# A low-rank decode-attention kernel: longer rows per load, a two-chunk ring, tapered last loads and an early softmax phase

## The chip, the cores and the metric

The kernel runs on one core of a Trainium2 chip. The metric is device time in microseconds (us). The kernel before takes 337.39 us (median of 6 runs, 337.14 to 338.04). A profile covers the span from the first to the last instruction, which is some 1.8 us shorter than the measured time. Engine names in the profile: PE is TensorE (matmuls), PEld its weight loads, DVE is VectorE, ACT is ScalarE, POOL is GpSimd, SP is SyncE; a "q" after a name is that engine's sequencer, for example while it issues a DMA. The granted PE clock is the share of TensorE's full clock that the profile records as granted.

## The reference, cut to what matters

```
B, H, Sq, Skv, Dh, R = 1, 16, 1, 8192, 256, 16          # everything in bf16
kp = einsum("rn,bhnd->bhrd", e_proj, k)                  # [16 heads, 16, 256]
vp = einsum("rn,bhnd->bhrd", f_proj, v)
scores = einsum("bhqd,bhrd->bhqr", q, kp) * (Dh ** -0.5)
p = softmax(scores, axis=-1)                             # over 16 values
o = einsum("bhqr,bhrd->bhqd", p, vp)
```

K and V are 67.1 MB each, and every byte is used once. Everything else is small: after the two projections only 16 x 256 numbers are left per head.

## The kernel before

Partition p holds positions n = 64 p to 64 p + 63 of a head, so a head of K is a tile of 128 partitions by 64 "columns" of 256 numbers, and one partition's 64 columns are 32 KB in one piece of memory. A chunk is some of these columns. Each column is one matmul (128 x 16 weights from e_proj, 128 x 256 of K).

```
CC_MAIN = 16        # columns per chunk: a 1 MB load with 8 KB per partition
CC_LAST = 8         # last head: 512 KB, 4 KB per partition
NB = 10             # ten K buffers and ten V buffers
...
# SP issues K (ACT issues V in the same way)
for i, (h, c0, c1) in enumerate(chunks):
    b = i % NB
    if i >= NB:
        sp.wait_ge(sem_kd, i - NB + 1)          # TensorE is done with this buffer
    sp.dma_start(kbuf[b][:, 0:(c1 - c0) * D], kv_src(kt, h, c0, c1)).then_inc(semK[b], 16)
...
# TensorE: K chunk, V chunk, K chunk, ...; after the last of them
pe.wait_ge(sem_dve, 7)                          # the softmax of all 16 heads is there
pe.wait_ge(sem_dvv, H)
for h in range(H):                              # 16 output matmuls
    mm = pe.matmul(ps_o[0:H, :], ptm[0:R, h * H:(h + 1) * H], vp_bf[0:R, h * D:(h + 1) * D],
                   start=(h == 0), stop=(h == H - 1))
...
# VectorE: one multiply-and-reduce with q per head, then once for all heads: transpose, max,
# scale, (exp on ScalarE), reciprocal, multiply, transpose, product with a block mask
```

## Time and profile before

| | before |
|---|---|
| measured median | 337.39 us |
| span of the profile | 335.6 us |
| PE busy | 241.1 us (72%) |
| bytes read | 134.87 MB, 421 GB/s from 20 to 240 us |
| mean granted PE clock | 0.987 |

From the page of the kernel before: the span, and three lines of the strip of 40 equal slices (busy tenths of PE, granted PE clock in tenths, GB/s that the DMA engines moved).

```profile
span 335.6 us, 4413 instructions
PE   0767867767767767866866787766866866867875
PEclk9998999999999999999999899999999999999999
GB/s 220 422 422 419 422 419 422 422 419 422 419 422 421 420 422 419 422 419 423 422 421 421 418 423 419 422 419 422 422 419 423 419 422 424 418 420 408 411 338 7
```

PE is never full and its clock is almost always granted. The load rate is flat at 418 to 424 GB/s from the second slice to the 36th, then 408 to 411 in the last head, whose rows are 4 KB long instead of 8 KB. That is the picture of a kernel bound by its load stream.

The end of the chain that ended last, in order of time (start us, us, what):

```profile
297.12 29.81 DMA vbuf<-in_v_dram
326.94 0.04 issue
326.98 1.04 PE vp_ps L206 x8
328.02 0.87 PE kp_ps L194 x8
328.89 0.89 PE vp_ps L206 x8
...
329.80 0.37 ACT vp_bf L157
330.18 0.30 ACT e L176 x2
...
331.51 1.92 PE ps_o L217 x16
333.43 0.02 issue
333.45 0.37 ACT o_sb L182
```

The chain leaves the DMA at 326.94 us. Then come three groups of eight matmuls, the softmax, 16 output matmuls, a copy, and the store to 335.6.

### The profile page before, as it was taken

To read this page: it belongs to the slowest core of one execution; us is meant where nothing else is said; L and a number is where in the kernel's file an instruction comes from. 1 tells how busy PE (TensorE), PEld (TensorE's weight loads), DVE (VectorE), ACT (ScalarE), POOL (GpSimd) and SP (SyncE) were. 2 spreads that over 40 slices of the span, in tenths; PEclk is the share of its full clock that TensorE was granted. 3 is DMA by queue.
4 is the path that set the end of the run, shared out by engine and by line. 5 is a ranking of instruction groups with operands and counts; after the bars stand their busy time and mean duration, and the time that the engine had idled before them with its cause. 6 is when DMAs were issued, how large, how long until landed. Compare 5 with 4: busy or idle time off the path is not lost.

```text
span 335.6 us, 4413 instructions
## 1 busy us (share of the span) xinstructions
PE 241.1 (72%) x2064; PEld 182.5 (54%) x2064; DVE 10.2 (3%) x45; ACT 8.1 (2%) x21; POOL 1.6 (0%) x6
## 2 busy tenths in 40 slices
PE   0767867767767767866866787766866866867875
PEld 0554655555655655655655565655655645656653
DVE  2000000000000000000000000000000000000002
ACT  0100000000000000000000000000000000000001
POOL 1000000000000000000000000000000000000000
PEclk9998999999999999999999899999999999999999
DMA  8999999999999999999999999999999999999980
GB/s 220 422 422 419 422 419 422 422 419 422 419 422 421 420 422 419 422 419 423 422 421 421 418 423 419 422 419 422 422 419 423 419 422 424 418 420 408 411 338 7
DMA packets 23793, 135.16 MB, mean 403 GB/s; under 512 B 6336, under 2 KB 6352, under 8 KB 8400
## 3 DMA queue, kind: packets, MB, share of 16 engines
q1 hardware_dynamic: 11920, 67.51, 49.0%
q10 hardware_dynamic: 11856, 67.38, 48.8%
q8 instruction: 16, 0.26, 0.3%
q14 instruction: 1, 0.01, 0.0%
HBM read 134.87 MB, written 0.01 MB: 402 GB/s over the span
## 4 chain that ended last, share of the span: by engine, by line
DMA 91%; PE 6%; ACTq 1%; ACT 0%; issue 0%; DVE 0%
DMA vbuf<-in_v_dram 91%; PE vp_ps L206 5%; ACTq L168 1%; PE kp_ps L194 1%; PE ps_o L217 1%; ACTq L149 0%; ACT vp_bf L157 0%; ACT o_sb L182 0%; ACT e L176 0%; DVE ptm L262 0%; DVE p L257 0%; DVE pt L259 0%; DVE stats L255 0%; ACTq L156 0%
## 5 line engine op out<-in xcount | busy, mean ns | idle before, releaser
L206 PE MATMUL vp_ps<-vbuf,f_sb 128*16 128x256 bf16 x1024 | 125.5, 276 | 80.6 <-DMA vbuf<-in_v_dram 80.6
L206 PEld LDWEIGHTS vp_ps<-vbuf,f_sb 128*16 128x16 bf16 x1024 | 87.9, 90 | 117.2 <-DMA vbuf<-in_v_dram 78.3
L194 PE MATMUL kp_ps<-kbuf,e_sb 128*16 128x256 bf16 x1024 | 125.4, 276 | 10.0 <-DMA kbuf<-in_k_dram 10.0
L194 PEld LDWEIGHTS kp_ps<-kbuf,e_sb 128*16 128x16 bf16 x1024 | 93.3, 91 | 31.0 <-issue 9.9
L238 DVE CUSTOM_DVE_ANT_0 junk<-kp_ps,q_bc 16x256 f32<-16x256 f32 x16 | 6.6, 412 | 314.4 <-PE kp_ps L194 314.4
L157 ACT ACTIVATE vp_bf<-vp_ps 16x256 bf16<-16x256 f32 x16 | 6.0, 373 | 309.1 <-PE vp_ps L206 309.1
L217 PE MATMUL ps_o<-vp_bf,ptm 16*16 16x256 bf16 x16 | 1.9, 268 | 1.7 <-DVE ptm L262 1.7
L217 PEld LDWEIGHTS ps_o<-vp_bf,ptm 16*16 16x16 bf16 x16 | 1.3, 85 | 2.4 <-DVE ptm L262 2.0
L171 ACT ACT_TABLE_LOAD x1 | 1.3, 1283 | 13.6 <-issue 13.6
L232 DVE COPY e_sb<-e_raw 128x1024 bf16<-128x1024 bf16 x1 | 1.0, 1027 | 5.3 <-DMA f_raw<-in_f_proj_dram 5.3
L238 DVE DVE_READ_ACCUMULATOR2_ANT s<- 16x1 f32 x16 | 1.1, 71 | 0.0
L233 DVE COPY f_sb<-f_raw 128x1024 bf16<-128x1024 bf16 x1 | 1.0, 1023 | 0.0
L113 POOL MEMSET maskbd<- 32x1024 bf16 x1 | 0.9, 941 | 0.3 <-POOLq L281 0.3
L115 POOL TENSOR_SCALAR_AFFINE_SELECT maskbd<-maskbd 16x256 bf16<-16x256 bf16 x1 | 0.5, 496 | 0.2 <-POOL maskbd L113 0.2
L182 ACT ACTIVATE o_sb<-ps_o 16x256 bf16<-16x256 f32 x1 | 0.4, 373 | 3.0 <-PE ps_o L217 3.0
L176 ACT ACTIVATE e<-st,stats 16x16 f32<-16x16 f32 x1 | 0.3, 290 | 0.0
L262 DVE TENSOR_TENSOR ptm<-maskbd,pt 16x256 bf16<-16x256 bf16 x1 | 0.3, 278 | 0.0
L257 DVE TENSOR_SCALAR p<-e,stats 16x16 bf16<-16x16 f32 x1 | 0.2, 222 | 0.0
L171 ACT ACTIVATE warm<-warm 1x1 f32<-1x1 f32 x1 | 0.2, 202 | 0.0
L259 DVE STREAM_TRANSPOSE pt<-p 32x32 bf16<-32x32 bf16 x1 | 0.2, 200 | 0.0
L249 DVE STREAM_TRANSPOSE st<-s 32x32 f32<-32x32 f32 x1 | 0.2, 199 | 0.0
L176 ACT ACTIVATION_READ_ACCUMULATOR e<-st,stats 16x1 f32 x1 | 0.2, 185 | 0.0
(11 smaller groups left out, 1.1 us busy)
## 6 DMA issues: line engine op xcount, KB each, us to landing
vbuf<-in_v_dram ACTq DMA_DIRECT2D x60, 1024.0 KB, 48.0
kbuf<-in_k_dram SPq DMA_DIRECT2D x60, 1024.0 KB, 47.5
kbuf<-in_k_dram SPq DMA_DIRECT2D x8, 512.0 KB, 37.2
vbuf<-in_v_dram ACTq DMA_DIRECT2D x8, 512.0 KB, 36.0
e_raw<-in_e_proj_dram SPq DMA_DIRECT2D x1, 256.0 KB, 3.9
f_raw<-in_f_proj_dram ACTq DMA_DIRECT2D x1, 256.0 KB, 5.4
q_bc<-in_q_dram SPq DMA_DIRECT2D x1, 128.0 KB, 5.7
out_dram<-o_sb SPq DMA_DIRECT2D x1, 8.0 KB, 1.4
```

Source lines behind the costliest of these rows:

```text
L113: gp.memset(mask[:], 0.0).then_inc(sem_mask, 1)
L115: gp.affine_select(out=mask[0:R, 0:H * H], in_=mask[0:R, 0:H * H], pattern=[[1, H], [-1, H]], compare_op=ALU.not_equal, fill=1.0, base=0, ...
L157: act.activation(vp_bf[0:R, h * D:(h + 1) * D], vp_ps[h % 2][:, :], ACT.Copy,).then_inc(sem_dvv, 1)
L168: act.dma_start(vbuf[b][:, 0:(c1 - c0) * D], kv_src(vt, h, c0, c1)).then_inc(semV[b], 16)
L171: act.activation(warm[0:1, 1:2], warm[0:1, 0:1], ACT.Exp)
L176: act.activation(e32[0:H, 0:R], st32[0:H, 0:R], ACT.Exp, bias=stats[0:H, 1:2], scale=scale, accum_out=stats[0:H, 2:3],).then_inc(sem_exp, 1)
L194: mm = pe.matmul(kp_ps[hb][:, :], e_sb[:, c, :], kbuf[b][:, (c - c0) * D:(c - c0 + 1) * D], start=(c == 0), stop=(c == C - 1),)
L206: mm = pe.matmul(vp_ps[hb][:, :], f_sb[:, c, :], vbuf[b][:, (c - c0) * D:(c - c0 + 1) * D], start=(c == 0), stop=(c == C - 1),)
L217: mm = pe.matmul(ps_o[0:H, :], ptm[0:R, h * H:(h + 1) * H], vp_bf[0:R, h * D:(h + 1) * D], start=(h == 0), stop=(h == H - 1),)
L232: dve.tensor_copy(e_sb[:], e_raw[:].transpose([0, 2, 1]))
L233: dve.tensor_copy(f_sb[:], f_raw[:].transpose([0, 2, 1])).then_inc(sem_prep, 1)
L238: dve.tensor_tensor_reduce(out=junk[hb][:, :], in0=kp_ps[hb][:, :], in1=q_bc[:, h * D:(h + 1) * D], scale=1.0, scalar=0.0, op0=ALU.mult, o ...
```

## The change

Its intent has two parts. The stream: load whole heads (64 columns, 4 MB, 32 KB per partition) for heads 0 to 11, in a ring of 160 columns for K and another for V, where two 64-column chunks fit. The tail: taper the loads of the last four heads, down to four columns for the last V; run softmax and output for heads 0 to 14 while the last head still loads; and fold the scaling by 1/sum into the last copy.

The diff, cut to its core:

```diff
-CC_MAIN = 16
-CC_LAST = 8
-NB = 10
+CC_MAIN = 64
+K_TAIL = {12: [32, 32], 13: [32, 32], 14: [32, 16, 16], 15: [16, 16, 16, 16]}
+V_TAIL = {12: [32, 32], 13: [32, 32], 14: [32, 16, 16], 15: [16, 16, 8, 8, 8, 4, 4]}
+RING = 160
+NS = 10
+K_AT = {(15, 48): (15, 36)}      # TensorE takes K's last chunk before V's chunk at column 40
...
+    hbs = [H - 1, H] if H > 1 else [H]        # two phases: heads 0-14, then all 16
...
-        kbuf = [sb([P, CCMAX * D], bf16, f"kbuf{b}") for b in range(NB)]
+        kbuf = sb([P, RING * D], bf16, "kbuf")
...
-                    if i >= NB:
-                        sp.wait_ge(sem_kd, i - NB + 1)
-                    sp.dma_start(kbuf[b][:, 0:(c1 - c0) * D], kv_src(kt, h, c0, c1)).then_inc(semK[b], 16)
+                    if kneed[i]:                          # chunks that overlapped this place are consumed
+                        sp.wait_ge(sem_kd, kneed[i])
+                    sp.dma_start(kbuf[:, koff[i] * D:(koff[i] + c1 - c0) * D],
+                                 kv_src(kt, h, c0, c1)).then_inc(semK[i % NS], 16)
...
+                    # TensorE, after V's first chunk of head 15: the output matmuls of heads 0-14
+                    while state["phased"] < NPH - 1 and h >= hbs[state["phased"]] and c0 == 0:
+                        emit_final(state["phased"], last=False)
+                        state["phased"] += 1
...
-                act.activation(o_sb[0:H, :], ps_o[0:H, :], ACT.Copy).then_inc(sem_oc, 1)
+                act.activation(
+                    o_sb[0:H, :], ps_o[0:H, :], ACT.Copy, scale=stats[NPH - 1][0:H, 2:3],
+                ).then_inc(sem_oc, 1)
```

More of the change, by code (lines that the diff above doesn't have):

```diff
@@ L35, in bass_standalone__low_rank_proj_linformer__decode_kernel, with make, place @@
     scale = float(D) ** -0.5
-    chunks = []
-    for h in range(H):
-        cc = CC_LAST if h == H - 1 else CC_MAIN
-        cc = min(cc, C)
-        assert C % cc == 0
-        for c0 in range(0, C, cc):
-            chunks.append((h, c0, c0 + cc))
-    NCH = len(chunks)
-    CCMAX = max(c1 - c0 for (_, c0, c1) in chunks)
-    end_cnt = {}
-    for i, (h, c0, c1) in enumerate(chunks):
-        if c1 == C:
-            end_cnt[h] = i + 1
-    assert NB <= NCH
+    def make(tails):
+        out = []
+        for h in range(H):
+            c0 = 0
+            for cc in tails.get(h, [CC_MAIN] * (C // CC_MAIN)):
+                out.append((h, c0, c0 + cc))
+                c0 += cc
+            assert c0 == C
+        return out
+    def place(chunks):
+        offs, need, off = [], [], 0
+        for i, (h, c0, c1) in enumerate(chunks):
+            n = c1 - c0
+            if off + n > RING:
+                off = 0
+            dep = max([j + 1 for j in range(i)
+                       if offs[j] < off + n and off < offs[j] + chunks[j][2] - chunks[j][1]],
+                      default=0)
+            offs.append(off)
+            need.append(max(dep, i - NS + 1, need[-1] if need else 0))
+            off += n
+        return offs, need
+    kch, vch = make(K_TAIL), make(V_TAIL)
+    koff, kneed = place(kch)
+    voff, vneed = place(vch)
+    kend = {h: i + 1 for i, (h, c0, c1) in enumerate(kch) if c1 == C}
+    vend = {h: i + 1 for i, (h, c0, c1) in enumerate(vch) if c1 == C}
+    order = []
+    ki = vi = 0
+    while vi < len(vch):
+        if ki < len(kch) and K_AT.get(kch[ki][:2], kch[ki][:2]) <= vch[vi][:2]:
+            order.append(("k", ki))
+            ki += 1
+        else:
+            order.append(("v", vi))
+            vi += 1
+    hbs = [H - 1, H] if H > 1 else [H]
     qt, kt, vt, et, ft, ot = (q.tensor, k.tensor, v.tensor,
@@ L63, in sm @@
             return es.enter_context(nc.semaphore(name))
+        NPH = len(hbs)
         e_raw = sb([P, R, C], bf16, "e_raw")
@@ L72, in bass_standalone__low_rank_proj_linformer__decode_kernel @@
         s32 = sb([32, 32], f32, "s32")
-        st32 = sb([32, 32], f32, "st32")
-        e32 = sb([32, 32], f32, "e32")
-        p16 = sb([32, 32], bf16, "p16")
-        pt16 = sb([32, 32], bf16, "pt16")
-        mask = sb([32, 32 * 32], bf16, "maskbd")
-        ptm = sb([32, 32 * 32], bf16, "ptm")
-        stats = sb([32, 4], f32, "stats")
+        stx = [sb([32, 32], f32, f"st{p}") for p in range(NPH)]
+        ex = [sb([32, 32], f32, f"e{p}") for p in range(NPH)]
+        etx = [sb([32, 32], f32, f"et{p}") for p in range(NPH)]
+        ptm = [sb([32, H * H], bf16, f"ptm{p}") for p in range(NPH)]
+        mask = sb([32, H * H], bf16, "maskbd")
+        stats = [sb([32, 4], f32, f"stats{p}") for p in range(NPH)]
         warm = sb([32, 2], f32, "warm")
         o_sb = sb([32, D], bf16, "o_sb")
-        kbuf = [sb([P, CCMAX * D], bf16, f"kbuf{b}") for b in range(NB)]
-        vbuf = [sb([P, CCMAX * D], bf16, f"vbuf{b}") for b in range(NB)]
+        kbuf = sb([P, RING * D], bf16, "kbuf")
+        vbuf = sb([P, RING * D], bf16, "vbuf")
         kp_ps = [ps([R, D], f32, f"kp_ps{b}") for b in range(2)]
         vp_ps = [ps([R, D], f32, f"vp_ps{b}") for b in range(2)]
-        ps_o = ps([R if R >= H else H, D], f32, "ps_o")
+        ps_o = ps([32, D], f32, "ps_o")
         sem_ef = sm("sem_ef")
@@ L94, in bass_standalone__low_rank_proj_linformer__decode_kernel @@
         sem_dvv = sm("sem_dvv")
-        sem_dve = sm("sem_dve")
-        sem_exp = sm("sem_exp")
+        sem_dx = [sm(f"sem_d{p}") for p in range(NPH)]
+        sem_ex = [sm(f"sem_e{p}") for p in range(NPH)]
         sem_peo = sm("sem_peo")
@@ L99, in bass_standalone__low_rank_proj_linformer__decode_kernel @@
         sem_out = sm("sem_out")
-        semK = [sm(f"semK{b}") for b in range(NB)]
-        semV = [sm(f"semV{b}") for b in range(NB)]
+        semK = [sm(f"semK{b}") for b in range(NS)]
+        semV = [sm(f"semV{b}") for b in range(NS)]
         def kv_src(tensor, h, c0, c1):
@@ L134, in _ @@
                 ).then_inc(sem_q, 16)
-                for i, (h, c0, c1) in enumerate(chunks):
-                    b = i % NB
-                    if i >= NB:
-                        sp.wait_ge(sem_kd, i - NB + 1)
-                    sp.dma_start(kbuf[b][:, 0:(c1 - c0) * D], kv_src(kt, h, c0, c1)).then_inc(semK[b], 16)
+                for i, (h, c0, c1) in enumerate(kch):
+                    if kneed[i]:
+                        sp.wait_ge(sem_kd, kneed[i])
+                    sp.dma_start(kbuf[:, koff[i] * D:(koff[i] + c1 - c0) * D],
+                                 kv_src(kt, h, c0, c1)).then_inc(semK[i % NS], 16)
                 sp.wait_ge(sem_oc, 1)
@@ L152, in _ @@
                 ).then_inc(sem_ef, 16)
-                copied = 0
+                state = {"copied": 0, "phased": 0}
                 def emit_vp_copy(h):
-                    act.wait_ge(sem_vd, end_cnt[h])
+                    act.wait_ge(sem_vd, vend[h])
                     act.activation(
@@ L159, in emit_vp_copy @@
                     ).then_inc(sem_dvv, 1)
-                for i, (h, c0, c1) in enumerate(chunks):
-                    b = i % NB
-                    if i >= NB:
-                        act.wait_ge(sem_vd, i - NB + 1)
-                        while copied < H and end_cnt[copied] <= i - NB + 1:
-                            emit_vp_copy(copied)
-                            copied += 1
-                    act.dma_start(vbuf[b][:, 0:(c1 - c0) * D], kv_src(vt, h, c0, c1)).then_inc(semV[b], 16)
-                    if i == NB - 1:
-                        act.wait_ge(sem_prep, 1)
-                        act.activation(warm[0:1, 1:2], warm[0:1, 0:1], ACT.Exp)
@@ L172, in _, with emit_exp @@
-                while copied < H:
-                    emit_vp_copy(copied)
-                    copied += 1
-                act.wait_ge(sem_dve, 3)
-                act.activation(
-                    e32[0:H, 0:R], st32[0:H, 0:R], ACT.Exp,
-                    bias=stats[0:H, 1:2], scale=scale,
-                    accum_out=stats[0:H, 2:3],
-                ).then_inc(sem_exp, 1)
-                act.wait_ge(sem_peo, 1)
-                act.activation(o_sb[0:H, :], ps_o[0:H, :], ACT.Copy).then_inc(sem_oc, 1)
+                def emit_exp(pi):
+                    hb = hbs[pi]
+                    act.wait_ge(sem_dx[pi], 2)
+                    act.activation(
+                        ex[pi][0:hb, 0:R], stx[pi][0:hb, 0:R], ACT.Exp,
+                        bias=stats[pi][0:hb, 0:1], scale=1.0,
+                        accum_out=stats[pi][0:hb, 1:2],
+                    ).then_inc(sem_ex[pi], 1)
@@ new lines, in emit_ready_work @@
+                def emit_ready_work(cnt):
+                    while state["copied"] < H and vend[state["copied"]] <= cnt:
+                        emit_vp_copy(state["copied"])
+                        state["copied"] += 1
+                    while state["phased"] < NPH - 1 and state["copied"] >= hbs[state["phased"]]:
+                        emit_exp(state["phased"])
+                        state["phased"] += 1
+                warmed = False
+                for i, (h, c0, c1) in enumerate(vch):
+                    if vneed[i]:
+                        if not warmed:
+                            act.wait_ge(sem_prep, 1)
+                            act.activation(warm[0:1, 1:2], warm[0:1, 0:1], ACT.Exp)
+                            warmed = True
+                        act.wait_ge(sem_vd, vneed[i])
+                        emit_ready_work(vneed[i])
+                    act.dma_start(vbuf[:, voff[i] * D:(voff[i] + c1 - c0) * D],
+                                  kv_src(vt, h, c0, c1)).then_inc(semV[i % NS], 16)
@@ L184, in _ @@
+                emit_ready_work(vend[H - 2])
+                emit_exp(NPH - 1)
+                emit_vp_copy(H - 1)
+                act.wait_ge(sem_peo, 1)
+                act.wait_ge(sem_dx[NPH - 1], 5)
+                act.activation(
+                    o_sb[0:H, :], ps_o[0:H, :], ACT.Copy, scale=stats[NPH - 1][0:H, 2:3],
+                ).then_inc(sem_oc, 1)
             @block.tensor
@@ L186, in _ @@
                 pe.wait_ge(sem_prep, 1)
-                for i, (h, c0, c1) in enumerate(chunks):
-                    b = i % NB
-                    hb = h % 2
-                    if c0 == 0 and h >= 2:
-                        pe.wait_ge(sem_dvk, h - 1)
-                    pe.wait_ge(semK[b], 16 * (i // NB + 1))
-                    for c in range(c0, c1):
-                        mm = pe.matmul(
-                            kp_ps[hb][:, :],
-                            e_sb[:, c, :],
-                            kbuf[b][:, (c - c0) * D:(c - c0 + 1) * D],
-                            start=(c == 0),
-                            stop=(c == C - 1),
-                        )
-                    mm.then_inc(sem_kd, 1)
+                state = {"phased": 0}
@@ new lines, in emit_final @@
+                def emit_final(pi, last):
+                    h0 = hbs[pi - 1] if pi > 0 else 0
+                    hs = list(range(h0, hbs[pi]))
+                    pe.wait_ge(sem_dx[pi], 4)
+                    pe.wait_ge(sem_dvv, hbs[pi])
+                    mm = None
+                    for h in hs:
+                        mm = pe.matmul(
+                            ps_o[0:H, :],
+                            ptm[pi][0:R, h * H:(h + 1) * H],
+                            vp_bf[0:R, h * D:(h + 1) * D],
+                            start=(h == 0), stop=(h == H - 1),
+                        )
+                    if last:
+                        mm.then_inc(sem_peo, 1)
@@ new lines, in _ @@
+                for kind, i in order:
+                    h, c0, c1 = (kch if kind == "k" else vch)[i]
+                    hb = h % 2
+                    if kind == "k":
+                        if c0 == 0 and h >= 2:
+                            pe.wait_ge(sem_dvk, h - 1)
+                        pe.wait_ge(semK[i % NS], 16 * (i // NS + 1))
+                        for c in range(c0, c1):
+                            o = (koff[i] + c - c0) * D
+                            mm = pe.matmul(kp_ps[hb][:, :], e_sb[:, c, :], kbuf[:, o:o + D],
+                                           start=(c == 0), stop=(c == C - 1))
+                        mm.then_inc(sem_kd, 1)
+                        continue
@@ L202, in _ @@
                     if c0 == 0 and h >= 2:
                         pe.wait_ge(sem_dvv, h - 1)
-                    pe.wait_ge(semV[b], 16 * (i // NB + 1))
+                    pe.wait_ge(semV[i % NS], 16 * (i // NS + 1))
                     for c in range(c0, c1):
-                        mm = pe.matmul(
-                            vp_ps[hb][:, :],
-                            f_sb[:, c, :],
-                            vbuf[b][:, (c - c0) * D:(c - c0 + 1) * D],
-                            start=(c == 0),
-                            stop=(c == C - 1),
-                        )
@@ L213, in _ @@
-                    mm.then_inc(sem_vd, 1)
-                pe.wait_ge(sem_dve, 7)
-                pe.wait_ge(sem_dvv, H)
-                for h in range(H):
-                    mm = pe.matmul(
-                        ps_o[0:H, :],
-                        ptm[0:R, h * H:(h + 1) * H],
-                        vp_bf[0:R, h * D:(h + 1) * D],
-                        start=(h == 0), stop=(h == H - 1),
-                    )
-                mm.then_inc(sem_peo, 1)
+                        o = (voff[i] + c - c0) * D
@@ new lines, in _ @@
+                        mm = pe.matmul(vp_ps[hb][:, :], f_sb[:, c, :], vbuf[:, o:o + D],
+                                       start=(c == 0), stop=(c == C - 1))
+                    mm.then_inc(sem_vd, 1)
+                    while state["phased"] < NPH - 1 and h >= hbs[state["phased"]] and c0 == 0:
+                        emit_final(state["phased"], last=False)
+                        state["phased"] += 1
+                while state["phased"] < NPH:
+                    emit_final(state["phased"], last=(state["phased"] == NPH - 1))
+                    state["phased"] += 1
@@ L227, in _ @@
                 dve.memset(s32[:], 0.0)
-                dve.memset(p16[:], 0.0)
-                dve.memset(stats[:], 0.0)
+                for pi in range(NPH):
+                    dve.memset(ex[pi][:], 0.0)
+                for pi in range(NPH):
+                    dve.memset(stats[pi][:], 0.0)
                 dve.memset(warm[:], 0.0)
@@ L234, in _, with emit_ttr @@
                 dve.wait_ge(sem_q, 16)
-                for h in range(H):
+                def emit_ttr(h):
                     hb = h % 2
-                    dve.wait_ge(sem_kd, end_cnt[h])
+                    dve.wait_ge(sem_kd, kend[h])
                     dve.tensor_tensor_reduce(
@@ L241, in _ @@
                         in1=q_bc[:, h * D:(h + 1) * D],
-                        scale=1.0,
+                        scale=scale,
                         scalar=0.0,
@@ L247, in _ @@
                     ).then_inc(sem_dvk, 1)
-                dve.wait_ge(sem_dvk, H)
-                dve.transpose(st32[:], s32[:]).then_inc(sem_dve, 1)
-                dve.wait_ge(sem_dve, 1)
-                dve.tensor_reduce(stats[0:H, 0:1], st32[0:H, 0:R], AX.X, ALU.max).then_inc(sem_dve, 1)
-                dve.wait_ge(sem_dve, 2)
-                dve.tensor_scalar_mul(stats[0:H, 1:2], stats[0:H, 0:1], -scale).then_inc(sem_dve, 1)
-                dve.wait_ge(sem_exp, 1)
-                dve.reciprocal(stats[0:H, 3:4], stats[0:H, 2:3]).then_inc(sem_dve, 1)
@@ L256, in _, with emit_phase @@
-                dve.wait_ge(sem_dve, 4)
-                dve.tensor_scalar_mul(p16[0:H, 0:R], e32[0:H, 0:R], stats[0:H, 3:4]).then_inc(sem_dve, 1)
-                dve.wait_ge(sem_dve, 5)
-                dve.transpose(pt16[:], p16[:]).then_inc(sem_dve, 1)
-                dve.wait_ge(sem_dve, 6)
-                dve.wait_ge(sem_mask, 2)
-                dve.tensor_tensor(
-                    ptm[0:R, 0:H * H],
-                    mask[0:R, 0:H * H],
-                    bass.AP(tensor=pt16, offset=0, ap=[[32, R], [0, H], [1, H]]),
-                    ALU.mult,
-                ).then_inc(sem_dve, 1)
+                def emit_phase(pi):
+                    ha, hb = 0, hbs[pi]
+                    dve.wait_ge(sem_dvk, hb)
+                    dve.transpose(stx[pi][:], s32[:]).then_inc(sem_dx[pi], 1)
+                    dve.wait_ge(sem_dx[pi], 1)
+                    dve.tensor_reduce(stats[pi][ha:hb, 0:1], stx[pi][ha:hb, 0:R], AX.X, ALU.max,
+                                      negate=True).then_inc(sem_dx[pi], 1)
+                    dve.wait_ge(sem_ex[pi], 1)
+                    dve.transpose(etx[pi][:], ex[pi][:]).then_inc(sem_dx[pi], 1)
+                    dve.wait_ge(sem_dx[pi], 3)
+                    dve.wait_ge(sem_mask, 2)
+                    nh = hb - ha
+                    dve.tensor_tensor(
+                        ptm[pi][0:R, ha * H:hb * H],
+                        mask[0:R, ha * H:hb * H],
+                        bass.AP(tensor=etx[pi], offset=0, ap=[[32, R], [0, nh], [1, H]]),
+                        ALU.mult,
+                    ).then_inc(sem_dx[pi], 1)
+                    dve.reciprocal(stats[pi][ha:hb, 2:3], stats[pi][ha:hb, 1:2]).then_inc(sem_dx[pi], 1)
@@ L271 @@
+                phased = 0
+                for h in range(H):
+                    emit_ttr(h)
+                    if phased < NPH - 1 and h + 1 == hbs[phased]:
+                        emit_phase(phased)
+                        phased += 1
+                while phased < NPH:
+                    emit_phase(phased)
+                    phased += 1
 _INS = ['q', 'k', 'v', 'e_proj', 'f_proj']
```

## The prediction

> **What bounds the kernel.** The load stream. In the 40-slice strip DMA is 9 tenths busy and moves 419-422 GB/s; the chain of waits is 91% "DMA vbuf"; PE is 72% busy and waits only for V. So the time is stream plus tail: the last V chunk lands at 326.94 us (timeline, chain), the span ends at 335.6. The median, 337.39 us, is 1.8 above the span.
>
> **Stream.** In steady state a K+V pair (2 x 1 MB, 8 KB rows) comes each 4.974 us, 16 packets for each of 16 engines: 310.9 ns a packet. In the last head (4 KB rows) a pair comes each 2.55 us: 159.4 ns. The difference, 151.5 ns for 4 KB, is 27.0 B/ns, or 433 GB/s on 16 engines, and leaves about 8 ns that a packet costs whatever its size. The packet records agree: 309-312 and 159-162 ns. [...] The change loads heads 0-11 with 32 KB rows: I estimate 1,220 ns a packet, 430 GB/s, 19.52 us a head in place of 19.90: 4.55 us over 12 heads. Heads 12-15 give another 0.9. Sum about 5.5 us; last landing near 321.4.
>
> **Does the shallower ring starve the stream?** Ten buffers become two 64-column chunks per queue, 8 MB. Matmuls come each 109 ns (16 take 1.74 us start to start), so 7.0 us a chunk and 14.0 us per K+V against 19.5 us of loading: V's next load is issued some 5 us before its queue runs dry, and a full queue can cover for the other. PE idles about 5 us per head. [...] here the first 16 matmuls after the idle start took 3.45 us against 1.91. [...] PE starts near 25 us instead of 10; harmless.
>
> **Tail.** Before, from the last landing: 2.8 us of matmuls, then softmax, scaling, transpose and mask to 331.5, 16 matmuls 1.92, copy 0.37, then 1.8 to store: 8.7 us in all. The change does 15 heads' part early, ends V with 4-column chunks, and folds the normalisation into the last copy. If the queues alternate packets, as the equal pace of K and V suggests, K's larger packets land K about 2.8 us before the last V. PE then still has 40 columns and ends some 1.6 us after the last landing. Then copy 0.4, one matmul 0.3, copy 0.4, store 1.8: about 4.8 us. Head 15's softmax (1.6 us after K's last matmul) hides behind V's matmuls. Gain about 4 us.
>
> **Time.** 337.4 - 5.5 - 4 = 328.0 us; range 325.5 to 331.5. Faster by over 2% (below 330.6): 0.85; same 0.14; slower 0.01.
>
> **What would show each step.** Slices at 428-432 GB/s for heads 0-11, falling toward 420 at the end; large packets near 1.21 us; landings 19.5 us apart; last V landing near 321.4; span end 4-5.5 us after it; PE clock mean 0.8-0.9; fifteen ps_o matmuls early, one last.
>
> **What would make it wrong.** 32 KB rows split into 8 KB packets or slower HBM reads (no stream gain: 333-334, "same"); half clock lasting, so that PE needs over 19.5 us a head and both queues run dry; large packets delaying the small e/f ones at the start; PE backlog in the tail over 3 us.

That a full queue can cover for the other is seen in the kernel before: V's first packet starts at 7.82 us, and from 7.0 to 7.8 us K's queue alone moved 410 GB/s.

## More of the kernel before

From the view of DMA issues of the kernel before (tile, issuer, count, KB each, median us from issue to landing), and the mean over a stretch of its middle (busy us of PE, PEld, DVE, ACT, POOL with instruction counts, then PE clock, DMA share, GB/s):

```profile
vbuf<-in_v_dram ACTq DMA_DIRECT2D x60, 1024.0 KB, 48.0
20.00:240.00 220.00, 162.57 (x1397) 123.72 (x1394) 4.62 (x22) 4.11 (x11) 0.00 (x0) 0.98 1.01 421
```

Every load waits 48 us in its queue behind nine others: there is always work for the DMA engines.

## The result

The changed kernel takes 328.58 us (median of 8 runs, 328.36 to 328.63). The ratio to before is 0.9736, with a 95% interval of 0.9726 to 0.9745; ratios here are the mean time of one kernel's fast runs over that of the other's fast runs of the same rounds, so not quite the ratio of the medians quoted. It is faster by 8.8 us.

The same lines of the page for the changed kernel:

```profile
span 326.6 us, 4336 instructions
PE   0009939699695988959599793997959999669995
PEclk9999978979797797989879798797989999979999
GB/s 253 405 450 438 419 425 446 436 401 444 434 444 409 446 427 425 431 446 421 415 446 423 438 423 446 417 427 433 429 417 423 431 427 419 434 413 420 419 392 59
```

Single slices now swing between 401 and 450 GB/s, because a whole 32 KB packet is booked where it starts: with each packet's bytes spread over its recorded time, slices 2 to 30 read 428 to 432. The mean over the middle is the number to read (same view and columns as before):

```profile
vbuf<-in_v_dram ACTq DMA_DIRECT2D x12, 4096.0 KB, 25.9
20.00:240.00 220.00, 177.29 (x1408) 135.18 (x1408) 4.62 (x22) 4.10 (x11) 0.00 (x0) 0.89 1.00 431
```

The rate is 431 GB/s in place of 421, with the DMA engines busy all the time in both (DMA share 1.00 and 1.01). PE's clock is 0.89 there in place of 0.98. The timeline of PE for one head shows why (start us, us, engine, line, op, tile, shape, count, idle time before it):

```profile
104.11 9.82 PE L261 MATMUL kp_ps<-kbuf,e_sb 128*16 128x256 bf16 x64 [3.62 <-DMA kbuf<-in_k_dram]
113.77 7.15 PE L270 MATMUL vp_ps<-vbuf,f_sb 128*16 128x256 bf16 x64
```

After 3.62 us of idling, the 64 K matmuls take 9.82 us; the 64 V matmuls that follow take 7.15. The clock record of the trace has half clock from 102.80 to 109.63 us. Shorter idle times were followed by half-rate matmuls as well: in the kernel before, 16 matmuls took 3.23 us in place of 1.91 after an idle time of 2.40 us, and in the changed kernel 32 took 5.00 in place of 3.66 after 2.73 us (3.41 us at half clock in the clock record each time), while after 2.55 us in the same kernel 32 took 3.66. So the length of the last idle time alone does not decide it; what does is not shown here.

The end of the chain of the changed kernel:

```profile
275.64 43.21 DMA kbuf<-in_k_dram
318.85 0.04 issue
318.90 1.91 PE kp_ps L261 x16
320.81 2.63 PE vp_ps L270 x24
323.44 0.02 issue
323.47 0.38 ACT vp_bf L190
323.85 0.14 issue
323.98 0.28 PE ps_o L243
324.26 0.02 issue
324.29 0.47 ACT o_sb L227
```

The chain now leaves the DMA at K's last chunk, not at V's; V's last four chunks (24 columns) have landed by the time PE comes to them. From K's last landing PE needs 4.6 us for the 40 columns that are left, and the rest 3.1 us. Only one output matmul is left at the end.

**When the last load really landed.** The chain shows a DMA only where an engine stood waiting for it. If the engine was still busy when the load landed, the chain runs through the engine instead. The semaphore records of the trace give every landing, one entry for each of the 16 DMA engines. For the last V chunk they say (us from the span's start):

```
            first engine   last engine    PE's last V matmul ends   span end
before          324.68        328.51             329.8               335.6
after           317.94        321.57             323.4               326.6
```

So the last load before landed at 328.51 us, not at 326.94. The gain of 9.0 us in the span splits into 6.9 us of stream (328.51 to 321.57) and 2.1 us of tail (7.1 to 5.0 us from the last landing to the end). The table also shows something that the prediction did not consider: the sixteen DMA engines finish 3.6 to 3.8 us apart.

### The profile page after: what moved, and what is told of

It is laid out like the page before. It is cut to its first block, busy times and chain, and to the rows that moved or that the text cites. A ratio compares the mean times of both kernels' runs of the same rounds, so it can differ in the third digit from the quotient of the medians.

```text
span 326.6 us, 4336 instructions
## 1 busy us (share of the span) xinstructions
PE 253.1 (77%) x2064; PEld 194.9 (60%) x2064; DVE 11.0 (3%) x50; ACT 8.6 (3%) x23; POOL 1.0 (0%) x6
## 4 chain that ended last, share of the span: by engine, by line
DMA 79%; PE 19%; SPq 1%; issue 0%; ACT 0%
DMA kbuf<-in_k_dram 79%; PE kp_ps L261 18%; PE vp_ps L270 1%; SPq L164 0%; SPq L171 0%; ACT o_sb L227 0%; SPq L160 0%; ACT vp_bf L190 0%; PE ps_o L243 0%
## 5 line engine op out<-in xcount | busy, mean ns | idle before, releaser
L261 PE MATMUL kp_ps<-kbuf,e_sb 128*16 128x256 bf16 x1024 | 140.3, 306 | 70.6 <-DMA kbuf<-in_k_dram 70.6
L261 PEld LDWEIGHTS kp_ps<-kbuf,e_sb 128*16 128x16 bf16 x1024 | 101.4, 100 | 108.2 <-issue 65.2
L270 PE MATMUL vp_ps<-vbuf,f_sb 128*16 128x256 bf16 x1024 | 115.5, 273 | 0.0
L270 PEld LDWEIGHTS vp_ps<-vbuf,f_sb 128*16 128x16 bf16 x1024 | 92.2, 90 | 19.6
L319 DVE TENSOR_TENSOR ptm<-maskbd,et 16x240 bf16<-16x240 bf16 (+1 forms) x2 | 0.8, 404 | 0.1
```

What stands on the lines that cost most here:

```text
L261: mm = pe.matmul(kp_ps[hb][:, :], e_sb[:, c, :], kbuf[:, o:o + D], start=(c == 0), stop=(c == C - 1))
L270: mm = pe.matmul(vp_ps[hb][:, :], f_sb[:, c, :], vbuf[:, o:o + D], start=(c == 0), stop=(c == C - 1))
L319: dve.tensor_tensor(ptm[pi][0:R, ha * H:hb * H], mask[0:R, ha * H:hb * H], bass.AP(tensor=etx[pi], offset=0, ap=[[32, R], [0, nh], [1, H]] ...
```

## The experiments

The theories. A packet is here one entry of the profile's DMA records, one contiguous piece: a row (one partition's part) of a load, unless the destination has gaps (the changed kernel's 24 loads of 128 rows of 32 KB are 3072 packets). Each load also sends a 4 B packet on each engine that tells of its completion (848 in the changed kernel for 53 loads and stores, as many as there are landings); the records give it 9 ns. **A**: every packet costs some 9 ns besides its bytes, so longer rows make the stream shorter. Its rivals are **B** (the tail alone gained) and **C** (fewer, larger loads gained, whatever their rows). For the tail: the early phase, the tapered chunks and a backlog of TensorE each have a share to be measured. **F**, formed after the first results: the engines finish apart because TensorE's own instructions come through them.

Here is what all runs gave, so that the sections below can be short. "Last landing" is the last engine's landing of the last V chunk, from the semaphore records of the run's profile; "tail" is the span's end less that. The profiles of e2, e5, e7 and e8, which ran together, were taken a second time, and only the second is kept: the last two columns are read from it, while the lines quoted for e5 and the slow run of e2 are of the first. The kernel before ran again beside each group of experiments, and each ratio is to those runs.

```
kernel                     median us  ratio to before [95%]      last landing   tail
before                      337.39                                  328.51       7.1
after                       328.58    0.9736 [0.9726, 0.9745]       321.57       5.0
e1_rows8k                   333.97    0.9897 [0.9879, 0.9915]       327.70       4.3
e2_rows16k                  329.76    0.9777 [0.9761, 0.9793]       323.73       4.9
e2b_rows16k                 329.69    0.9767 [0.9743, 0.9791]       323.16       4.7
e3_4mb_8k                   332.90    0.9865 [0.9847, 0.9883]       326.41       4.6
e4_one_softmax              330.10    0.9780 [0.9764, 0.9795]       321.70       6.5
e5_even_tail                329.09    0.9760 [0.9744, 0.9777]       322.05       5.5
e9_stream_only              331.06    0.9811 [0.9788, 0.9834]       321.91       7.2
e6_fine_tail                327.31    0.9699 [0.9683, 0.9714]       321.77       3.8
e12_best                    331.04    0.9809 [0.9781, 0.9836]       321.52       7.6
e7_warm                     329.93    0.9785 [0.9771, 0.9800]       323.28       5.0
e10_half_matmuls (wrong)    325.07    0.9632 [0.9611, 0.9653]       319.64       3.6
e8_data_first               328.81    0.9751 [0.9736, 0.9765]       322.00       4.9
```

All gave correct results but e10. Its output is wrong, which doesn't matter for the time. All runs were fast but one of e2, whose median includes it (its ratio does not).

### Rows of 8 KB with the new tail (e1_rows8k)

```diff
-CC_MAIN = 64
-K_TAIL = {12: [32, 32], 13: [32, 32], 14: [32, 16, 16], 15: [16, 16, 16, 16]}
-V_TAIL = {12: [32, 32], 13: [32, 32], 14: [32, 16, 16], 15: [16, 16, 8, 8, 8, 4, 4]}
+CC_MAIN = 16
+K_TAIL = {}
+V_TAIL = {15: [16, 16, 8, 8, 8, 4, 4]}
```

> The changed kernel with every head but the last cut into 16-column chunks again (1 MB loads, 8 KB rows, ten of them in the ring); the new tail stays. Theory A (long rows save a fixed cost of some 9-10 ns per packet): the stream falls back to about 421 GB/s and the time rises by 5.5 to 7 us over the changed kernel, to about 334.5 us. Rival B (the whole gain is in the tail; the shorter stream is a by-product): the time stays near 328.6 us.

Measured: 333.97 us, 5.4 us over the changed kernel. The middle of this kernel, in the view of a stretch:

```profile
20.00:240.00 220.00, 162.57 (x1397) 123.65 (x1394) 4.63 (x22) 4.10 (x11) 0.00 (x0) 0.98 1.01 421
```

The rate is back at 421 GB/s, and the last landing is 6.1 us later than in the changed kernel. B falls.

### Loads of 4 MB with packets of 8 KB (e3_4mb_8k)

The ring gets a gap of 32 B after every 16 columns, so that the rows of a load can't be joined into one piece; sizes of loads, waits and order stay.

```diff
-        kbuf = sb([P, RING * D], bf16, "kbuf")
+        GW = GRP * D + GAP                                   # GRP = 16 columns, GAP = 16 numbers
+        kbuf = sb([P, RING // GRP, GW], bf16, "kbuf")
...
-                ap=[[C * D, P], [1, (c1 - c0) * D]],
+                ap=([[C * D, P], [GRP * D, n // GRP], [1, GRP * D]] if n > GRP
+                    else [[C * D, P], [1, n * D]]),
...                                                          # destination and matmul operands likewise
```

> The changed kernel with the same 4 MB and 2 MB loads and the same two-chunk ring, but with a gap of 32 B after every 16 columns of the ring, so that each row of a load goes out as pieces of 8 KB. Theory A (cost per packet): only the semaphore packets are saved, about 0.9 us of the gain; time near 333.5 us, packets of 8 KB at about 310 ns. Rival C (what saves time is fewer, larger loads, whatever their packets): time stays at 328.6 us.

Measured: 332.90 us. From the view of a stretch of this kernel:

```profile
20.00:240.00 220.00, 173.13 (x1399) 133.45 (x1399) 4.63 (x22) 3.73 (x10) 0.00 (x0) 0.91 1.01 422
```

The packet records have the 8 KB pieces, 312 ns each (median), and as many as in e1. Loads four times as large, with the same two-chunk ring, move 422 GB/s, which is what 1 MB loads move. C falls but for a small part: this kernel is 1.1 us faster than e1, and it sends 82 fewer completion packets per engine (one per load and engine), which at their recorded 9 ns are 0.7 us. What counts is the length of the piece that goes out as one packet, which in the other kernels is the row.

### Rows of 16 KB (e2_rows16k, e2b_rows16k)

```diff
-CC_MAIN = 64
+CC_MAIN = 32
```

> The changed kernel with heads 0 to 11 in 32-column chunks (2 MB loads, 16 KB rows). Theory A (a fixed cost of about 10 ns per packet, with its share of semaphore packets): 32 packets of 16 KB per engine and head in place of 16 of 32 KB cost 16 x 10 ns x 12 heads = 1.9 us: 330.5 us, that is one third of the way from 32 KB rows (328.6) to 8 KB rows (334.0). Rival (any row over 8 KB does, or the gain comes only at full 32 KB contiguous rows): 328.6 or 334.

The first profile of this kernel fell into a run of 501.36 us in which TensorE was 97% busy: its matmuls followed each other at some 233 ns (256 in 59.7 us), where 109 ns is usual, although its record has the granted clock at 1.00 throughout. The other three runs took 329.5 to 329.9 us. Why that one run was slow stays open; but it shows what happens when TensorE needs more than the loads do. The same kernel was run again:

> The kernel with 32-column chunks (16 KB rows) once more, unchanged: its first profile fell into a run of 501 us in which TensorE ran at half pace from start to end, and gave no fast profile. Theory A: 1.8 us over the changed kernel (330.4 us), packets of 16 KB at 611 to 614 ns; the three fast runs of the first time had 329.5 to 329.9. Expected now: 329.5 to 330.5 us, slices at 425 to 429 GB/s.

Measured: 329.69 us, last landing 323.16, and from 20 to 240 us

```profile
20.00:240.00 220.00, 174.60 (x1438) 132.19 (x1436) 4.62 (x22) 4.11 (x11) 0.00 (x0) 0.94 1.01 427
```

With 8, 16 and 32 KB rows the rates are 421, 427 and 431 GB/s. Counting packets gives the cost: e1 sends 656 more data packets per engine than the changed kernel (8 for each of 82 more chunks) and lands 6.13 us later, 9.3 ns each; e2b sends 192 more (8 for each of 24 more chunks) and lands 1.59 us later, 8.3 ns each. Both figures include the completion packets; e3, which has the 656 packets more without them, lands 4.84 us later, 7.4 ns each. The packet records say the same from the other side: 159, 309, 611 and 1213 ns, the shortest that the changed kernel has for 4, 8, 16 and 32 KB, are all within 2 ns of 8 ns plus 150.7 ns for each 4 KB. A stands. In time the 16 KB kernel lost 1.1 us, not the expected 1.8: its tail is 0.3 us shorter, and medians of different chips are compared, which the intervals (0.0024 of 337 us is 0.8 us) allow for.

### The tail of before with the new stream (e9_stream_only)

This is the changed kernel with one phase and with K and V of the last head in eight chunks of eight columns.

```diff
-    hbs = [H - 1, H] if H > 1 else [H]
+    hbs = [H]
-K_TAIL = {..., 15: [16, 16, 16, 16]}
+K_TAIL = {..., 15: [8] * 8}                # V_TAIL likewise; K_AT = {}
```

> The changed kernel with the long rows and the two-chunk ring, but with the tail of before: one softmax after the last K, 16 output matmuls at the end, K and V of the last head in eight chunks of 8 columns. Theory: against the kernel before only the stream is shorter, by some 5.4 us (what the 8 KB rows took away from the changed kernel), and nearly the whole tail of about 7 us from the last landing stays, less the folded steps: 331 us. If stream and tail add up, this gain and that of the 8 KB-row kernel (3.4 us) together give the 8.8 us of the change.

Measured: 331.06 us. The last landing is 321.91 and the tail is 7.2 us, as before the change. The stream alone gained 6.3 us and the tail alone (e1) 3.4; together that is 9.7, while the change gained 8.8. About 0.6 of the missing 0.9 us is the same new tail, which takes 5.0 us behind 32 KB rows but 4.3 behind 8 KB rows; the rest lies in the landings and stays open. TensorE is not further behind with longer chunks: in the changed kernel, e1, e2b, e3 and e4 alike it waits for K's last chunk and ends 4.58 us after its landing. But that landing comes 3.4 us before V's last in e1, 3.0 in e2b and 2.7 in the changed kernel. With these chunks it is K's last landing that sets the end.

The folded scaling has no visible part in the gain. From K's last matmul to the mask product it shortens the softmax from 2.6 us (before) to 2.0 (e9), but in the changed kernel that stretch ends 0.6 us before V's last matmul.

### One softmax phase (e4_one_softmax), and even last chunks (e5_even_tail)

e4 makes only the `hbs = [H]` edit. e5 makes only the edit of the last head's chunk sizes.

> The changed kernel without the early phase: one softmax over 16 heads after the last K, and all 16 output matmuls after it; the tail chunks stay. Theory: TensorE's last V matmul still ends some 4.5 us after the last K chunk lands, the softmax hides behind it, and 16 output matmuls in place of 1 add about 1.65 us: 330.2 us. Rival (the early phase is worth the whole tail gain of the prediction, 4 us): 332.5 us.

Measured: 330.10 us. The timeline of its end:

```profile
324.04 1.90 PE L243 MATMUL ps_o<-vp_bf,ptm 16*16 16x256 bf16 x16 [0.55 <-ACT vp_bf L190]
325.98 0.46 ACT L227 ACTIVATE o_sb<-ps_o,stats 16x256 bf16<-16x256 f32 x1 [2.08 <-PE ps_o L243]
```

Sixteen output matmuls in 1.90 us stand where the changed kernel has one in 0.28 us. The early phase is worth 1.5 us, and it is these matmuls: the softmax itself was hidden in both.

> The changed kernel with both K and V of the last head in eight chunks of 8 columns, as before the change; the early phase stays. Theory: K's last chunk now lands only some 0.4 us before V's, so the last head's softmax (1.9 us from K's last matmul to the mask product) is no longer hidden: TensorE ends 1.5 to 2 us after the last landing and the output waits another 0.5 to 1 us for the softmax; against that the backlog of 24 V columns is gone. Net 328 to 329.5 us. Rival (the uneven chunk sizes are what makes the tail short): 330 us or more.

Measured: 329.09 us, 0.5 over the changed kernel, where the intervals of the two ratios just touch. From its timeline:

```profile
324.09 0.41 DVE L319 TENSOR_TENSOR ptm<-maskbd,et 16x256 bf16<-16x256 bf16 x1
324.56 0.27 PE L243 MATMUL ps_o<-vp_bf,ptm 16*16 16x256 bf16 x1 [1.18 <-DVE ptm L319]
```

The last output matmul waits 1.18 us for the softmax of the last head (DVE, ptm), which is the price of K landing together with V. The uneven chunks remove that wait but leave more V columns to multiply after K, so the net is about half a microsecond, hardly clear of the noise.

### Finer last loads (e6_fine_tail)

In the changed kernel TensorE has 40 columns before it when K's last chunk lands at 318.85, and ends 1.9 us after V's last landing. Smaller K chunks were to let it start on them sooner, and smaller V packets to let K run further ahead.

```diff
-K_TAIL = {..., 15: [16, 16, 16, 16]}
-V_TAIL = {..., 15: [16, 16, 8, 8, 8, 4, 4]}
-K_AT = {(15, 48): (15, 36)}
+K_TAIL = {..., 15: [16, 16, 16, 8, 8]}
+V_TAIL = {..., 15: [8, 8, 8, 8, 8, 8, 4, 4, 4, 4]}
+K_AT = {(15, 16): (15, 8), (15, 32): (15, 16), (15, 48): (15, 24), (15, 56): (15, 32)}
```

> The changed kernel with finer last loads: K of the last head in 16,16,16,8,8 columns, V in 8,8,8,8,8,8,4,4,4,4, so that K runs further ahead of V. Theory (in the changed kernel TensorE holds a backlog of about 40 columns when K's last 16-column chunk lands, and ends about 1.9 us after V's last landing): the backlog shrinks to under 1 us after the last landing and the time falls by 1.5 to 2.2 us, to about 326.7 us. Rival (the tail is set by the last landing and the fixed copies and store): no change, 328.6 us, or slower by the smaller packets.

Measured: 327.31 us, faster than the changed kernel by 1.3 us (the intervals of the two ratios don't meet), a little less than the 1.5 to 2.2 expected. From its timeline:

```profile
317.82 1.04 PE L261 MATMUL kp_ps<-kbuf,e_sb 128*16 128x256 bf16 x8 [0.58 <-DMA kbuf<-in_k_dram]
318.69 3.72 PE L270 MATMUL vp_ps<-vbuf,f_sb 128*16 128x256 bf16 x32
321.81 0.32 PEld L270 LDWEIGHTS vp_ps<-vbuf,f_sb 128*16 128x16 bf16 x4 [0.18 <-DMA vbuf<-in_v_dram]
```

K's last eight columns start a microsecond sooner than K's last sixteen did, 3.95 us before V's last landing in place of 2.67, and the weight loads of the last four V columns now wait for their DMA: the backlog is gone, V's matmuls end 0.6 us after the last landing, and the tail is 3.8 us. This is the fastest correct kernel.

### The same with heads 12 and 13 in whole-head chunks (e12_best)

```diff
-K_TAIL = {12: [32, 32], 13: [32, 32], 14: [32, 16, 16], 15: [16, 16, 16, 8, 8]}
+K_TAIL = {14: [32, 16, 16], 15: [16, 16, 16, 8, 8]}      # V_TAIL likewise
```

> The fine tail (K 16,16,16,8,8 and V 8,8,8,8,8,8,4,4,4,4 in the last head), with heads 12 and 13 in 64-column chunks as well. Theory A: two more heads with 16 fewer packets each per engine save 0.3 us against the fine tail's 327.3 us: 327.0 us; TensorE catches up during head 14. Rival (the longer bursts of head 13 leave TensorE behind at the end): 327.5 us or more.

Measured: 331.04 us, 3.7 us slower than e6, although the last landing is 0.25 us earlier, as theory A has it. The timeline of PE, from the landing of head 13's K:

```profile
280.45 8.81 PE L261 MATMUL kp_ps<-kbuf,e_sb 128*16 128x256 bf16 x64 [3.63 <-DMA kbuf<-in_k_dram]
289.10 7.15 PE L270 MATMUL vp_ps<-vbuf,f_sb 128*16 128x256 bf16 x64
...
322.36 3.66 PE L270 MATMUL vp_ps<-vbuf,f_sb 128*16 128x256 bf16 x32
```

PE idles until 280.45 us for head 13, and from there it never waits for a load again: it ends at 326.0 us, 4.5 us after the last landing. My expectation that TensorE would catch up during head 14 was wrong, and the rival was right. Here half clock is no longer free: head 13's K burst takes 8.81 us in place of 7.15, and with no later wait to absorb them, these 1.7 us are an estimated part of the 3.7. The taper over heads 12 and 13 is not there for the stream, which it costs a little; it is there so that TensorE starts early on what has landed.

### TensorE kept busy (e7_warm)

```diff
...                                                      # ps_j, a spare accumulator, is allocated
                     mm.then_inc(sem_vd, 1)
+                    if c1 - c0 == CC_MAIN:
+                        for _ in range(40):             # into an accumulator that nobody reads
+                            pe.matmul(ps_j[:, :], e_sb[:, 0, :], f_sb[:, 0:D // R, :],
+                                      start=True, stop=True)
```

> The changed kernel with 40 matmuls into an unused accumulator after each V chunk of heads 0 to 11 (4.4 us of work per head, result unused), so that TensorE does not stand idle for 5 us per head. Theory (TensorE is off the critical path there; half clock costs nothing): the mean granted clock rises from 0.92 to 0.97 or more, the half-rate K bursts vanish, and the time stays within 0.3% of 328.6 us, perhaps 0.3 us longer for about four more instruction fetches of 16 KB. Rival (the half clock delays the release of the ring and so the stream): the time falls by 1 us or more.

Measured: the clock rises to 0.994, and the time is 329.93 us, 1.35 us longer. The rival falls: half clock does not hold up the stream (431 GB/s from 20 to 240 us at a DMA share of 1.00 in the changed kernel, 430 to 432 here). But the size of the loss missed my expectation (0.3% at most), and that led to theory F. The queue that carries instructions, in the page's list of DMA queues (packets, MB, share of 16 engines), has in the changed kernel

```profile
q8 instruction: 16, 0.26, 0.3%
```

and in this one

```profile
q8 instruction: 20, 0.33, 0.4%
```

The packet records give 1.02 to 1.11 us for nearly every one of these 16 KB packets, and a data packet right behind each one that took some 0.5 us longer than its like. In the landings of the last V chunk, eight engines of this kernel stand at 318.27 to 318.96 us, five at 321.36 to 321.64 and three at 322.85 to 323.28; in the changed kernel eight stand at 317.93 to 318.72 and eight at 321.03 to 321.57. Nineteen of the twenty fetches had begun by 306.4 us; the last began at 321.57 us, when the stream was all but over. So three fetches more than in the changed kernel could delay the loads, and three engines are later by about 1.5 us.

### Half the matmuls, with a wrong result on purpose (e10_half_matmuls)

```diff
-                        for c in range(c0, c1):
+                        for c in range(c0, c1, 2):          # K and V; stop at c == C - 2
```

> Wrong result on purpose: the changed kernel with the same loads, waits and order, but only every second column is multiplied, so TensorE has half as many instructions. Theory F (TensorE's own instructions arrive in 16 KB packets through the same DMA engines; each holds up one engine's data by some 1.5 us, eight of the sixteen engines get two each, and the stream ends with the slowest): 8 fetches in place of 16, the landings of one chunk spread over about 2 us in place of 3.6, and the last landing comes about 1.5 us sooner, near 320.0 us; the time falls by that and by the tail's backlog, about 2.4 us more: 324.5 to 326 us. Rival (the engines are unequal for another reason): spread stays at 3.6 us and the last landing at 321.6 us.

Measured: the page shows 2288 instructions in place of 4336, and the packet records eight fetches in place of sixteen. The engines' landings of the last V chunk lie 1.7 us apart in place of 3.6, and the last landing is 319.64 us, 1.9 us sooner, with the same loads. Here is how busy the DMA engines were microsecond by microsecond, first in the changed kernel and then in this one (columns as above, the DMA share is the last but one):

```profile
318.00:319.00 1.00, 0.17 (x2) 0.10 (x2) 0.00 (x0) 0.00 (x0) 0.00 (x0) 1.00 0.52 209
319.00:320.00 1.00, 1.00 (x11) 0.82 (x10) 0.00 (x0) 0.00 (x0) 0.00 (x0) 1.00 0.50 197
320.00:321.00 1.00, 1.00 (x12) 0.83 (x10) 0.15 (x1) 0.00 (x0) 0.00 (x0) 1.00 0.38 145
```

```profile
318.00:319.00 1.00, 1.00 (x9) 0.44 (x6) 0.78 (x4) 0.05 (x1) 0.00 (x0) 1.00 0.53 203
319.00:320.00 1.00, 0.73 (x5) 0.19 (x4) 0.58 (x3) 0.35 (x2) 0.00 (x0) 1.00 0.04 14
```

In the changed kernel half of the engines are done some 3 us before the others; with half the instructions that stretch is half as long. F is confirmed in both directions (20, 16 and 8 fetches; last landing 323.28, 321.57 and 319.64 us). With 5088, 4128 and 2080 matmuls and weight loads in the three kernels, that is one fetch for each 254 to 260 of them.

The landings of all V chunks, in order, show it step by step. In this kernel the sixteen engines land within 0.4 us of each other until the first fetch at 49.3 us. After it one engine is 1.7 us behind, after the second two, and so on to eight; in each of the 26 V chunks the number of late engines is the number of fetches so far. In e7 the first eight fetches put eight engines 1.6 to 2.0 us behind, and the ninth to sixteenth put the same number of engines about 3 us behind, one by one. In the changed kernel the count holds up to the fifth fetch and at the end; in between the engines also shift against each other for other reasons. So the fetches seem to go round the same eight engines. The records do not name them: this is read from the landings. A correct kernel with fewer TensorE instructions was not built, so what is to be gained there stays an estimate from these runs, about 1.5 to 2 us.

### The first K and V loads before the small ones (e8_data_first)

The edit moves the loads of e_proj, q and f_proj behind the first K and V load of their queue.

```diff
-                sp.dma_start(e_raw[:], ...).then_inc(sem_ef, 16)      # and q
                 for i, (h, c0, c1) in enumerate(kch):
                     ...
                     sp.dma_start(kbuf[:, ...], kv_src(kt, h, c0, c1)).then_inc(semK[i % NS], 16)
+                    if i == 0:
+                        sp.dma_start(e_raw[:], ...).then_inc(sem_ef, 16)      # and q; f_proj on ACT
```

> The changed kernel with the first K and V loads issued ahead of e_proj, f_proj and q. In the changed kernel the first 8 us move only 216 to 251 GB/s and V's first packet starts at 7.9 us though f_proj's last packet ended at 4.8 us. Theory D (that gap comes from V's load standing behind f_proj's 2048 small packets in its queue): the gap closes and the last landing comes about 1.2 us sooner, 327.4 us. Rival (the small packets cost their 3.3 us wherever they stand, and a gap comes after them anyway): no change, 328.6 us, or a loss of 1 us or more if the small packets wait for long ones and TensorE starts late.

Measured: 328.81 us, the same as the changed kernel within the noise, and a last landing 0.4 us later. V's first packet does start at 3.7 us instead of 7.9, so the gap closes, but the 128 B packets of e_proj and f_proj then break into the stream between 20 and 30 us (328 GB/s there), and the first matmul starts at 28.0 us instead of 25.0. No gain: theory D was right about the gap and wrong about its worth.

## Why the prediction was right

It said 328.0 us; measured were 328.58. Point by point:

- **The stream bounds the kernel, and row length sets its rate.** Right, and shown by e1, e2b and e3. The estimate was 1,220 ns for a 32 KB packet and 430 GB/s; the records say 1,213 to 1,221 ns and 431 GB/s. The predicted limit for very long rows, 433 GB/s (435 by the packet records: 150.7 ns for each 4 KB on 16 engines), stays an estimate from packet times: the longest rows that ran, 32 KB, gave 431.
- **Two terms were mis-sized, in opposite directions.** The step "the last V chunk lands at 326.94 us" was wrong: that was the last but one, and the last landed at 328.51, unseen because PE was still busy. So the old tail was 7.1 us, not "8.7 us in all"; the tail gained 2.1 us, not "about 4"; and the stream gained 6.9 us, not "about 5.5". The two misses, 1.4 and 1.9 us, nearly cancel in the total. The new last landing came out right (321.57, predicted 321.4) only because a start that was 1.6 us too early and a gain that was 1.4 us too small cancel: that is luck. The 5.0 us from there to the end (predicted 4.8) is not luck; it was summed from steps that the trace bears out. The lesson is about reading the old profile, not about the change.
- **Where the extra 1.4 us of stream comes from.** Of the 6.9 us, longer rows are 6.1 (e1 against the changed kernel), and 0.8 is left for the last head, whose rows were 4 KB before; its 40 packets and 5 completions fewer per engine would be some 0.4 us by an estimate from the 8 and 9 ns above, so half of that stays open. About 1 us of the extra 1.4 is in heads 0 to 11: a whole head takes 19.42 us from landing to landing of K in the changed kernel (predicted 19.52) against 19.88 before, so a head saves 0.46 us and not 0.38. The mis-sized term is the 32 KB packet, estimated at 1,220 ns: 16 of them, with two completions of 9 ns, in 19.42 us are 1,213 ns each.
- **The shallow ring does not starve the stream, and half clock is free in heads 0 to 11.** Right: the DMA share stays at 1.00, and e7 removed the half clock without gain. K bursts took 8.5 to 10 us in place of 7.15, so 1.3 to 2.8 us more, and K and V of a head together 15.5 to 17.0 us, against 19.42 of loading. (The mean clock of the profile was 0.916, a little over the forecast 0.8 to 0.9.) The 501 us run shows that the margin is real but finite: at 233 ns a matmul throughout, in place of 109, TensorE was 97% busy and became the bound.
- **The tail's order.** Right: K landed 2.7 us before V (predicted 2.8). The prediction took it that the queues alternate packets, and the packet records of the changed kernel have them so: sixteen 32 KB packets of K, as many as there are engines, start from 6.73 us, sixteen of V from 7.94, of K from 9.15, of V from 10.36, and so on. So the first K and V loads, eight rows per engine and a completion each, landed only two packets of 1.2 us apart, at 24.2 and 26.6 us. TensorE ended 1.9 us after the last landing (predicted 1.6); the last head's softmax was hidden. e6 shows that this backlog was not necessary.
- **Not foreseen:** the engines' unequal finish (F), with 16 fetches and a spread of 3.6 to 3.8 us in both kernels, so that it hardly touched the difference.

## What to carry to other kernels

When a kernel is bound by its load stream, count packets, not only bytes and loads: making each row four times as long took 2% off a stream that already used 1 MB loads, and the same 4 MB loads cut into short rows kept only a fifth of that (1.1 of 5.4 us). Long chunks must be tapered towards the end early enough for the consumer to catch up, since its unfinished work at the last landing is exposed in full (e12 lost in the tail fifteen times what it gained in the stream). And before splitting a profile into "stream" and "tail", look for the landing itself: a chain of waits shows a transfer only where somebody stood waiting for it.
